# Local attention with its scores in eight 64x32 tiles of the array, one score and one transpose stage per tile, and outputs normalised instead of probabilities

## The chip, the cores and the metric

The kernel runs on one core of one Trainium2 chip. The metric is the device time of one execution in microseconds (us), as the median of several executions. A core has five engines that run side by side and wait for each other by semaphores: TensorE (PE in the profile; PEld is its loading of weights), VectorE (DVE), ScalarE (ACT), GpSimd (POOL) and SyncE (SP), which here only issues transfers. TensorE writes its products to PSUM, which has eight banks; everything else lies in SBUF.

## The reference

Four batches of eight heads hold 512 local and 32 global tokens of 64 numbers each. A local query sees the 32 global keys and the local keys at most 32 places away. Two feed-forward layers follow, over all 2176 tokens of 512 numbers:

```python
s_ll = np.where(np.abs(pos[:, None] - pos[None, :]) <= 32, scale * q_l @ k_l.T, -1e9)
s_lg = scale * q_l @ k_g.T
a_l = softmax(concatenate([s_lg, s_ll], -1))       # e / (sum(e) + 1e-9), e = exp(s - max)
out_l = a_l @ concatenate([v_g, v_l])
out_g = softmax(scale * q_g @ concatenate([k_g, k_l]).T) @ concatenate([v_g, v_l])
x = concatenate([out_g, out_l])                     # as (2176, 512)
x = (h * clip(h + 3, 0, 6) / 6) @ w_out             # h = x @ w_in, d_ff = 2048; float64 weights
x = elu(x @ w_in2) @ w_out2                         # the same sizes
```

## The kernel before, in words

**Products.** The tokens are 17 tiles of 128: 16 of local queries and one that holds all global ones. They are handled in six chunks of 3, 3, 3, 2, 3 and 3 tiles (`CHUNKS`). For each chunk and each of 16 slots of 128 of d_ff there is an `up` product (12 matmuls into one bank `h`) and, two slots later, a `down` product in two parts (6 and 6 matmuls into the four banks `acc`). Every operand is a high and a low part (`gh` and `gl`, `x1h` and `x1l`), so a product is three matmuls. After `up`, ScalarE and VectorE make `g` out of `h` (L403, L404), ScalarE rounds it to `gh` (L409), and `gl` is the rest (L411, on GpSimd in the first chunk and on VectorE afterwards).

**Weights.** They come as float64, seen as two words. `Split` turns a slot `f` into two float32 parts: L100 on ScalarE, L104, L108 and L111 on VectorE, L121 on ScalarE, and two subtractions on GpSimd (L123). For the first layer this happens at the start and during the first chunk, for the second layer during the last chunk of the first. `tick` spreads these stages: two calls in a step of a slot, the first with L104 and L121 and L123, the second with L108, L111 and L100.

**Local attention.** `Local` does one tile of 128 queries and all eight heads in six stages: scores of two pairs of heads (S of part 0 and of part 1), transposes of the probabilities (T of part 0 and of part 1), the values (O) and the transposes of the output (XT). In S a matmul takes the queries of two heads, 32 of each, as 64 columns over all 128 rows of the array; the other head's rows hold zeros. VectorE adds the mask and takes the minimum of the negated scores (L218), ScalarE takes the exponential with a running sum (L222), VectorE adds 1e-9 to the sums and inverts them (L225, L226), and the probabilities are multiplied by that (L229): on VectorE for the first three tiles, on GpSimd for the others. T goes through PSUM and ScalarE (L239); O is 32 matmuls of 32 columns each, and ScalarE copies it to `x` (L256). XT is turned into `x1h` (L263, ScalarE) and `x1l` (L264, VectorE). `Global` does 32 global queries of four heads in three stages (SG; TG with Tg; OG).

**Order.** It is written out by hand, and every engine works off its own queue in that order. The attention of the first three tiles stands ahead of all products, mixed with loads and splitting by the string `PRO`. The tiles of chunk c+1 are done during chunk c, in the gaps between its products: three gaps in a step (after `up`, and after either part of `down`). `place` gives the stages of a job their places and `step` the distance to the next job; `during` spreads them over the gaps. All stages after the first three tiles use two PSUM banks (`att`) in turn: a stage waits until the one that used its bank two turns earlier has been read out.

**Transfers.** SyncE issues all of them in one queue. A load waits at the queue's head until its buffer is free: `qk` has one buffer, so the next tile's queries and keys are loaded after the scores, and the values `v` (two halves with tag `v`) after O. The raw weights share 16 buffers (tag `w`) with the operands of the first three tiles and the finished weights.

Of the kernel before, what the change touches and what calls it, by code (L numbers as in the profile page):

```python
# [14 lines left out]
ALU = mybir.AluOpType  # L15
# [27 lines left out]
# A float64's upper word, read as float32, has the upper 8 of its 11 exponent bits as its exponent;  # L43
# times this it has them less 896 = 1023 - 127.
# [9 lines left out]
def tile_kernel(ctx, tc, qkW, vW, qkG, vN, vG, masks, w1, w2, out):  # L54
# [10 lines left out]
    msk = pool.tile([P, 3, 2, P], F32, name="msk")  # L65
# [63 lines left out]
    def tick(m, times=1):  # L129
        """The next two stages of splitting the weights of layer m, of slots that follow each other."""  # L130
# [28 lines left out]
    class Local:  # L159
        """Attention of 128 local queries, all heads, cut into stages."""  # L160

        def __init__(self, n):
# [3 lines left out]
            self.p = {}  # L166

        def load_qk(self):
            tag, bufs = ("w", NF) if self.early else ("qk", 1)
            qk = pool.tile([P, 2, 2, 2 * P + WIN], F32, name=f"qk{self.n}", tag=tag, bufs=bufs)  # L170
# [10 lines left out]
        def load_v(self):  # L181
# [6 lines left out]
            for i in range(2):  # L188
                nc.sync.dma_start(self.v[i], src[:, i])
# [471 lines left out]
```

## Time and profile before

| what | value |
|---|---|
| runs | 923.87, 925.02 and 925.42 us, median 925.02 us |
| profiled execution | span 923.7 us; the profile has no other time for it |
| PE busy | 883.6 us (96%) |
| PEld, DVE, ACT, POOL busy | 811.8, 411.6, 424.1 and 183.6 us |
| the chain that ended last | PE 80%, DVE 10%, ACT 5%, issue 4%, POOL 1% |
| moved | 90.27 MB, mean 98 GB/s |

The busy times are sums over stages of different kinds, so they don't tell what ends a given stage; the chain follows the work back from the last instruction, at each step to what released it. "Issue" in it is time for which the profile shows no wait.

### The profile page before, as it was taken

How to read it: one execution, taken by the hardware profiler on the slowest of the kernel's cores; microseconds unless marked ns; L12 is line 12 of the kernel's file. 1: busy time of each engine (PE TensorE's matmuls, PEld its weight loads, DVE VectorE, ACT ScalarE, POOL GpSimd, SP SyncE). 2: the span in 40 equal slices, each digit the busy share in tenths (PEclk: the TensorE clock that was granted, in tenths of full speed). 3: DMA queues.
4: the chain of work that ended last, by engine and by line, in shares of the span. 5: the costliest groups of instructions: out<-in, count | busy, mean ns of one | idle time of the engine just before them, and what ended most of it. 6: DMA issues, size and time to landing. Idle time of an engine off the chain costs nothing.

```text
span 923.7 us, 15740 instructions
## 1 busy us (share of the span) xinstructions
PE 883.6 (96%) x6432; PEld 811.8 (88%) x6432; DVE 411.6 (45%) x911; ACT 424.1 (46%) x944; POOL 183.6 (20%) x124
## 2 busy tenths in 40 slices
PE   6588799999999999999999989999999999999998
PEld 4477799989989999999999979999999999989997
DVE  4988864332432343432339978432222232322222
ACT  5666645433532354443335566533443444434433
POOL 0489781100100010000006644300100101001000
PEclk9799899999999999999999989999999999999999
DMA  9766313331423235232056630020010020100100
GB/s 371 319 270 225 135 47 109 131 122 45 134 80 130 65 124 164 89 101 67 1 179 238 259 140 18 18 69 0 1 57 1 1 69 1 57 1 1 35 1 34
DMA packets 21816, 90.27 MB, mean 98 GB/s; under 512 B 2544, under 2 KB 5872, under 8 KB 17264
## 3 DMA queue, kind: packets, MB, share of 16 engines
q1 hardware_dynamic: 21744, 89.27, 27.1%
q8 instruction: 50, 0.82, 0.4%
q14 instruction: 22, 0.18, 0.1%
HBM read 80.35 MB, written 8.91 MB: 97 GB/s over the span
## 4 chain that ended last, share of the span: by engine, by line
PE 80%; DVE 10%; ACT 5%; issue 4%; POOL 1%; DMA 0%; ACTq 0%; DVEq 0%
PE acc L389 36%; PE h L389 36%; DVE f L108 4%; DVE f L111 3%; PE S L204 3%; DVE f L104 1%; PE O L248 1%; PE T L74 1%; DVE g L404 1%; ACT P L222 1%; PE SG L316 1%; ACT room L222 1%; PE OG L346 1%; ACT w L121 1%; ACT gh L409 0%
## 5 line engine op out<-in xcount | busy, mean ns | idle before, releaser
L389 PE MATMUL acc<-gh,w 128*128 128x384 f32 (+1 forms) x768 | 213.9, 337 | 0.0
L389 PE MATMUL h<-x1h,w 128*128 128x384 f32 (+1 forms) x768 | 209.6, 338 | 4.0 <-POOL w L123 2.8
L389 PE MATMUL h<-x2h,w 128*128 128x384 f32 (+1 forms) x768 | 203.5, 330 | 0.0
L389 PE MATMUL acc<-w,gh 128*128 128x512 f32 x544 | 171.9, 397 | 3.3 <-ACT ev L437 3.3
L409 ACT CAST gh<-g 128x384 fp32r<-128x384 f32 (+1 forms) x192 | 95.1, 495 | 153.9 <-DVE g L404 90.9
L389 PEld LDWEIGHTS h<-x1h,w 128*128 128x128 f32 x768 | 140.0, 191 | 10.1 <-POOL w L123 3.5
L389 PEld LDWEIGHTS acc<-gh,w 128*128 128x128 f32 x768 | 139.3, 189 | 5.0 <-issue 3.8
L389 PEld LDWEIGHTS h<-x2h,w 128*128 128x128 f32 x768 | 138.7, 189 | 4.1
L408 DVE SCALAR_TENSOR_TENSOR g<-g,h 128x384 f32<-128x384 f32 (+1 forms) x96 | 51.1, 532 | 199.2 <-ACT g L407 199.2
L389 PE MATMUL h<-x1l,w 128*128 128x384 f32 (+1 forms) x384 | 127.6, 332 | 4.5 <-DVE x1l L264 4.5
L411 DVE TENSOR_TENSOR gl<-g,gh 128x384 fp32r<-128x384 f32 (+1 forms) x176 | 95.6, 543 | 77.1 <-ACT gh L409 77.0
L389 PE MATMUL acc<-gl,w 128*128 128x384 f32 (+1 forms) x384 | 126.9, 330 | 2.6 <-POOL gl L411 2.6
L123 POOL TENSOR_TENSOR w<-f,w 128x512 fp32r<-128x512 f32 x64 | 110.9, 1753 | 89.7 <-ACT w L121 89.7
L389 PE MATMUL h<-x2l,w 128*128 128x384 f32 (+1 forms) x384 | 126.7, 330 | 0.0
L404 DVE SCALAR_TENSOR_TENSOR g<-g,h 128x384 f32<-128x384 f32 (+1 forms) x96 | 50.9, 530 | 154.7 <-ACT g L403 154.6
L389 PEld LDWEIGHTS acc<-w,gh 128*128 128x128 f32 x544 | 101.1, 190 | 19.4 <-ACT ev L437 3.6
L406 ACT ACTIVATE g<-h 128x384 f32<-128x384 f32 (+1 forms) x96 | 45.5, 474 | 145.2 <-PE h L389 145.2
L403 ACT ACTIVATE g<-h,half 128x384 f32<-128x384 f32 (+1 forms) x96 | 53.9, 562 | 119.2 <-PE h L389 116.5
L389 PE MATMUL acc<-w,gl 128*128 128x512 f32 x272 | 108.1, 398 | 0.0
L464 POOL TENSOR_TENSOR x2l<-x2raw,x2h 128x768 fp32r<-128x768 f32 (+1 forms) x12 | 21.9, 1823 | 325.2 <-ACT x2h L463 325.2
L229 POOL TENSOR_TENSOR P<-P,sums 128x512 f32<-128x512 f32 x26 | 31.2, 1198 | 246.0 <-DVE sums L226 221.3
L389 PEld LDWEIGHTS h<-x1l,w 128*128 128x128 f32 x384 | 73.3, 191 | 4.9 <-DVE x1l L264 4.9
(72 smaller groups left out, 918.8 us busy)
## 6 DMA issues: line engine op xcount, KB each, us to landing
raw<-in_w SPq DMA_DIRECT2D x32, 1024.0 KB, 6.7
qk<-in_qkW SPq DMA_DIRECT2D x15, 960.0 KB, 4.8
v<-in_vW SPq DMA_DIRECT2D x26, 512.0 KB, 4.9
qkG<-in_qkG SPq DMA_DIRECT2D x8, 608.0 KB, 3.8
vN<-in_vN SPq DMA_DIRECT2D x8, 512.0 KB, 4.7
out<-ev SPq DMA_DIRECT2D x16, 256.0 KB, 2.1
x2d<-ev SPq DMA_DIRECT2D x20, 192.0 KB, 2.1
x2raw<-x2d SPq DMA_DIRECT2D x10, 384.0 KB, 3.7
```

The source lines that it names most:

```text
L108: nc.vector.scalar_tensor_tensor(w, self.high[:, s], -0x80000000, w, op0=ALU.bitwise_and, op1=ALU.bitwise_or)
L111: nc.vector.scalar_tensor_tensor(w, self.low[:, s], 29, w, op0=ALU.logical_shift_right, op1=ALU.bitwise_or)
L123: nc.gpsimd.tensor_sub(lo[:, i], self.wf[:, i], hi[:, i].bitcast(F32))
L204: nc.tensor.matmul(sp[r : r + 64, j, i // 2, :], self.q[:, part, j, i, :], self.k[:, part, j, 32 * i : 32 * i + P], start=True, stop=True,)
L229: eng.tensor_tensor(pf, pf, sums.unsqueeze(2).to_broadcast([P, 4, P]), op=ALU.mult)
L389: nc.tensor.matmul(o, a, b, start=first and i == 0, stop=last and i == len(pairs) - 1)
L403: nc.scalar.activation(g, hp, AF.Relu, scale=1.0 / 6.0, bias=half)
L404: nc.vector.scalar_tensor_tensor(g, g, 1.0, hp, op0=ALU.min, op1=ALU.mult)
L406: nc.scalar.activation(g, hp, AF.Relu, scale=-1.0)
L408: nc.vector.scalar_tensor_tensor(g, g, -1.0, hp, op0=ALU.add, op1=ALU.max)
L409: nc.scalar.copy(gh, g)
L411: late.append(lambda: eng.tensor_sub(gl, g, gh.bitcast(F32)))
```

## The change

`Local` is rebuilt. In S each head has its own matmuls: its 64 rows of the array (upper or lower half) by 32 columns, for 32 queries, so that eight such tiles of the array can be filled; the outputs of the upper half go to one bank (`S_0`) and those of the lower half to another (`S_1`). The zeros between the heads are gone from the transfer of the queries, and the mask is half as large. A tile has one S stage with 32 matmuls over two banks, one T stage with eight transposes over two banks, O over two banks, and XT: four stages in place of six. V has a 65th column of ones, so the last column of O is the sum of the probabilities; the sums of L222 and the multiplications of L229 (L numbers of before) are gone, and VectorE takes the sums out of O (L235 of the changed kernel), inverts them (L236) and multiplies the outputs (L239), which replaces ScalarE's copy of O. The operands and probabilities of later tiles have one buffer each, the places are 0, 4, 6, 8 with a step of 9 (before 0, 2, 4, 7, 9, 11 with a step of 6), those of `Global` 0, 3, 5 (before 0, 4, 8), and `PRO` has a new order. The diff, cut to its core:

```diff
--- before.py
+++ after.py
-PRO = "q0 q1 v0 q2 v1 00 01 10 02 11 03 20 v2 12 04 13 21 05 W4 14 a100 a200 a101 W a201 a300 15 22 a110 a111 a301 a400 a210 a211 a310 23 w1 24 a311 a401 w1 q3 25 a410 a411 w1 w1 w1 | W | | | | | w1 w1 | w1 | w1 v3 |"
+PRO = "q0 q1 v0 q2 v1 00 v2 10 01 W4 20 11 02 a100 a200 a101 W a201 a300 21 03 12 a110 a111 a301 a400 a210 a211 a310 13 22 w1 23 a311 a401 w1 q3 a410 a411 w1 w1 w1 | W | | | | | w1 w1 | w1 | w1 v3 |"
...
     class Local:
...
         def __init__(self, n):
...
         def load_qk(self):
...
+            qk = pool.tile([P, NP, P + WIN], F32, name=f"qk{self.n}", tag=tag, bufs=bufs)
...
+                nc.sync.dma_start(qk[:, :2], src[:, :2])
...
+                nc.sync.dma_start(qk[:, 2:], src[:, 2:])
...
+            self.q, self.k = qk[:, :, :P], qk[:, :, P:]
...
         def load_v(self):
...
+            tag, bufs = ("w", NF) if self.early else ("vw", 1)
+            self.v = pool.tile([P, TPB, H, D + 1], F32, name=f"v{self.n}", tag=tag, bufs=bufs)
+            nc.sync.dma_start(self.v, vW[self.b, self.t])
+        def buffers(self):
...
+                room = pool.tile([P, 2, 2, NP, P], F32, name=f"room{self.n}", tag="w", bufs=NF)
+                return room[:, 0], room[:, 1]
+            p = pool.tile([P, 2, NP, P], F32, name=f"P{self.n}", tag="p", bufs=1)
+            pt = pool.tile([P, 2, NP, P], F32, name=f"PT{self.n}", tag="pt", bufs=1)
+            return p, pt
+        def scores(self, tag):
+            self.p, self.pt = self.buffers()
+            sp = [bank([P, NP, P], f"S{self.n}_{r}", tag) for r in range(2)]
+            mn = pool.tile([P, 2, NP], F32, name=f"mn{self.n}", tag="mn", bufs=2)
+            mi = 0 if self.t == 0 else (2 if self.t == TPB - 1 else 1)
+            for j in range(NP):
                 for i in range(4):
...
+                    for r in range(2):
+                        rs, cs = slice(64 * r, 64 * r + 64), slice(32 * i, 32 * i + 32)
+                        nc.tensor.matmul(
+                            sp[r][cs, j, :], self.q[rs, j, cs], self.k[rs, j, 32 * i : 32 * i + P],
+                            start=True, stop=True,
+                        )
+            for j in range(NP):
+                for r in range(2):
                     nc.vector.tensor_tensor_reduce(
...
+                        out=self.p[:, r, j, :], in0=sp[r][:, j, :], in1=msk[:, mi, :], scale=-SCALE, scalar=BIG,
+                        op0=ALU.add, op1=ALU.min, accum_out=mn[:, r, j : j + 1],
...
                     nc.scalar.activation(
...
+                        self.p[:, r, j, :], self.p[:, r, j, :], AF.Exp, scale=-1.0, bias=mn[:, r, j : j + 1]
...
+        def transposed(self, tag):
+            for r in range(2):
+                tp = bank([P, NP, P], f"T{self.n}_{r}", tag)
+                for j in range(NP):
+                    transpose(tp[:, j, :], self.p[:, r, j, :])
+                nc.scalar.copy(self.pt[:, r], tp)
+        def values(self, tag):
+            op = [bank([P, NP, D + 1], f"O{self.n}_{r}", tag) for r in range(2)]
+            sums = pool.tile([P, 2, NP], F32, name=f"sums{self.n}", tag="sums", bufs=2)
+            for r in range(2):
+                for j in range(NP):
+                    for i in range(4):
+                        cs = slice(32 * i, 32 * i + 32)
+                        nc.tensor.matmul(
+                            op[r][cs, j, :], self.pt[:, r, j, cs], self.v[:, i, 2 * j + r, :], start=True, stop=True
+                        )
+                nc.vector.tensor_scalar_add(sums[:, r], op[r][:, :, D], 1e-9)
             nc.vector.reciprocal(sums, sums)
...
+            self.x = pool.tile([P, NP, 2, D], F32, name=f"x{self.n}", tag="x", bufs=1)
+            for r in range(2):
+                nc.vector.tensor_tensor(
+                    self.x[:, :, r, :], op[r][:, :, :D], sums[:, r].unsqueeze(2).to_broadcast([P, NP, D]), op=ALU.mult
+                )
...
         def turned(self, tag):
...
+                transpose(xp[:, kd, :], self.x[:, kd].rearrange("p r d -> p (r d)"))
...
+        def stages(self, tags=("att",) * 4, nxt=None):
             def first():
...
+                self.scores(tags[0])
...
+            def third():
+                self.values(tags[2])
...
+            return [first, lambda: self.transposed(tags[1]), third, lambda: self.turned(tags[3])]
...
     class Global:
...
         def __init__(self, b, hf):
...
-            self.v = pool.tile([P, TPB, 4, D], F32, name=f"vN{g}", tag="v", bufs=2)
+            self.v = pool.tile([P, TPB, 4, D], F32, name=f"vN{g}", tag="vw", bufs=1)
-            self.p = pool.tile([P, S], F32, name=f"PG{self.g}", tag="p", bufs=2)
+            self.p = pool.tile([P, S], F32, name=f"PG{self.g}", tag="p", bufs=1)
...
-            self.pt = pool.tile([P, TPB, P], F32, name=f"PTG{self.g}", tag="pt", bufs=2)
+            self.pt = pool.tile([P, TPB, P], F32, name=f"PTG{self.g}", tag="pt", bufs=1)
...
-            place, step = ((0, 2, 4, 7, 9, 11), 6) if isinstance(job, Local) else ((0, 4, 8), 6)
+            place, step = ((0, 4, 6, 8), 9) if isinstance(job, Local) else ((0, 3, 5), 6)
-        first = [locs[n].stages(tags=("acc", "acc", "att", "att", "h", "h")) for n in range(CHUNKS[0])]
+        first = [locs[n].stages(tags=("acc", "att", "h", "acc")) for n in range(CHUNKS[0])]
...
-    qb = np.zeros((B, TPB, 2, D, NP, 4, 2, 32), q_l.dtype)
...
+    qb = q_l.reshape(B, NP, 2, TPB, P, D).transpose(0, 3, 2, 5, 1, 4).reshape(B, TPB, P, NP, P)
...
-    vW = c(vw.transpose(0, 3, 5, 1, 4, 2, 6))
...
+    vW = np.ones((B, TPB, P, TPB, H, D + 1), v_l.dtype)
+    vW[..., :D] = vw.transpose(0, 2, 4, 3, 1, 5)
```

On PE, in the second chunk, names are `h_<chunk>_<slot>` for `up`, `acc_<chunk>_<bank>` for `down`; here is the stretch from XT of one tile to S of another, before:

```order
L74 MATMUL XT_1735<-ident,x_1709 128x128 x4
L389 MATMUL h_1_5_1744<-x1h_907,w_5_631 128x384
...
L389 MATMUL h_1_5_1744<-x1h_907,w_5_631 128x384
L389 MATMUL acc_1_0_1554<-gh_1_3_1607,w_3_543 128x384
...
L389 MATMUL acc_1_1_1555<-gh_1_3_1607,w_3_543 128x384
L204 MATMUL S_0_1770<-qk_1649 64x128 x8
L389 MATMUL acc_1_2_1556<-gh_1_3_1607,w_3_543 128x384
```

and the stretch from XT of the first tile of that chunk's attention to S of the second in the changed kernel:

```order
L365 MATMUL h_1_3_1689<-x1h_789,w_3_589 128x384
L74 MATMUL XT_1708<-ident,x_1667 128x128 x4
L365 MATMUL acc_1_0_1673<-gh_1_1_1568,w_1_470 128x384
...
L365 MATMUL acc_1_1_1674<-gh_1_1_1568,w_1_470 128x384
L203 MATMUL S_0_1726<-qk_1539 32x128
L203 MATMUL S_1_1727<-qk_1539 32x128
...
L365 MATMUL acc_1_2_1675<-gh_1_1_1568,w_1_470 128x384
```

Between XT and the following S there stood 18 matmuls of the products (12 of `up`, 6 of `down`), and now stand 6; XT itself now comes directly behind `up`, and S uses two banks, of which `S_1` is the one that XT has just filled.

On DVE, in the first chunk, `f` is a slot being split and `g_0_<slot>` the activation; here are the instructions of one step before:

```order
L404 SCALAR_TENSOR_TENSOR g_0_5_739<-g_0_5_739,h_0_5_726 128x384
L104 TENSOR_SCALAR f_8_724<-f_8_724 128x1024
L218 ISA P_1_768,mn_1_769<-S_1_759,msk 128x128
L218 ISA mn_1_769 128x1
...
L225 TENSOR_SCALAR sums_1_770<-sums_1_770 128x4
L226 RECIPROCAL sums_1_770<-sums_1_770 128x4
L108 SCALAR_TENSOR_TENSOR f_8_724<-raw_8_571,f_8_724 128x1024
L111 SCALAR_TENSOR_TENSOR f_8_724<-raw_8_571,f_8_724 128x1024
```

and in the changed kernel the steps with S of the same tile, and with O of the tile ahead of it:

```order
L380 SCALAR_TENSOR_TENSOR g_0_5_810<-g_0_5_810,h_0_5_797 128x384
L104 TENSOR_SCALAR f_8_795<-f_8_795 128x1024
L209 ISA P_830,mn_834<-S_0_832,msk 128x128
...
L108 SCALAR_TENSOR_TENSOR f_8_795<-raw_8_617,f_8_795 128x1024
...
L104 TENSOR_SCALAR f_6_637<-f_6_637 128x1024
L235 TENSOR_SCALAR sums_700<-O_0_698 128x4
L235 TENSOR_SCALAR sums_700<-O_1_699 128x4
L236 RECIPROCAL sums_700<-sums_700 128x8
L239 TENSOR_TENSOR x_736<-O_0_698,sums_700 128x4x64
L239 TENSOR_TENSOR x_736<-O_1_699,sums_700 128x4x64
L108 SCALAR_TENSOR_TENSOR f_6_637<-raw_6_509,f_6_637 128x1024
```

The instruction on the sums, which stood between the scores and L108 of a slot and needs ScalarE's exponentials, has left that place; in its stead the sums and the multiplications stand behind O, ahead of L108 of another slot.

On SP, `raw_0_<slot>` is a slot's float64 weights; here is the queue around the second later tile's values, before:

```order
L83 DMA raw_9_629<-in_w 128x2048
L83 DMA raw_10_695<-in_w 128x2048
L83 DMA raw_11_745<-in_w 128x2048
L177 DMA qk_782<-in_qkW 128x1920
L189 DMA v_0_825<-in_vW 128x1024
L189 DMA v_1_826<-in_vW 128x1024
L83 DMA raw_12_852<-in_w 128x2048
```

and now:

```order
L83 DMA raw_9_678<-in_w 128x2048
L183 DMA v_739<-in_vW 128x2080
L83 DMA raw_10_764<-in_w 128x2048
L83 DMA raw_11_816<-in_w 128x2048
L177 DMA qk_883<-in_qkW 128x1408
L83 DMA raw_12_914<-in_w 128x2048
```

The values, whose load waits for O of the tile before, moved ahead of slots 10 and 11.

## Rows read from the trace of the kernel before

**Rows 1.** Busy time by stretch: span, engines (instructions), clock, DMA share, GB/s.

```profile
0.00:26.50 26.50, 15.98 (x254) 13.01 (x255) 12.46 (x69) 15.65 (x59) 0.70 (x6) 0.94 0.94 377
26.50:130.50 104.00, 82.46 (x721) 73.97 (x720) 90.54 (x131) 62.99 (x128) 81.80 (x50) 0.92 0.55 207
130.50:483.40 352.90, 351.87 (x3216) 328.87 (x3217) 125.28 (x442) 147.89 (x395) 28.64 (x26) 1.00 0.30 99
483.40:541.70 58.30, 54.98 (x314) 54.66 (x312) 53.53 (x53) 34.77 (x50) 34.19 (x19) 0.99 0.64 231
541.70:923.70 382.00, 378.27 (x1932) 341.32 (x1932) 129.80 (x217) 162.77 (x316) 38.26 (x24) 0.99 0.08 27
```

**Rows 2.** Waits of PE, 130.6 to 483.4: total us, times, longest.

```profile
PE XT L74 <- ACT PTG L335: 0.8, 1, 0.8
```

**Rows 3.** The chain that ended last, in order of time: start, us, engine, line.

```profile
136.94 2.11 PE h L389 x12
139.04 1.02 PE S L204 x16
140.07 2.31 PE acc L389 x12
...
147.82 0.44 PE T L74 x4
148.26 2.10 PE h L389 x12
...
161.68 1.03 PE O L248 x64
162.71 1.25 PE acc L389 x6
...
168.00 1.05 PE acc L389 x6
```

**Rows 4.** Waits of DVE, 44.5 to 128.4: total us, times, longest.

```profile
DVE sums L225 <- ACT P L222: 8.2, 6, 2.1
DVE x1l L264 <- ACT x1h L263: 2.3, 2, 1.3
```

**Rows 5.** DVE and POOL by line, 44.5 to 128.4: busy us, mean ns | idle before.

```profile
L226 DVE RECIPROCAL sums<-sums 128x4 f32<-128x4 f32 x6 | 1.1, 178 | 0.2
...
L229 POOL TENSOR_TENSOR P<-P,sums 128x512 f32<-128x512 f32 x6 | 9.8, 1626 | 3.0 <-DVE sums L226 2.0 <-ACT g L403 1.0
```

**Rows 6.** DVE and POOL by line, 130 to 483: the same columns.

```profile
L218 DVE CUSTOM_DVE_ANT_0 P<-S,msk 128x128 f32<-128x128 f32 x80 | 18.5, 287 | 5.5 <-PE S L204 5.4
...
L404 DVE SCALAR_TENSOR_TENSOR g<-g,h 128x256 f32<-128x256 f32 x16 | 6.7, 421 | 25.1 <-ACT g L403 25.1
...
L229 POOL TENSOR_TENSOR P<-P,sums 128x512 f32<-128x512 f32 x20 | 21.4, 1070 | 242.9 <-DVE sums L226 219.3 <-ACT PT L239 17.9 <-ACT x L256 4.2
```

**Rows 7.** Timeline of DVE and POOL: start, us, engine, line.

```profile
41.24 1.23 DVE L108 SCALAR_TENSOR_TENSOR f<-raw,f 128x1024 int32<-128x1024 int32 x1
92.84 1.88 DVE L108 SCALAR_TENSOR_TENSOR f<-raw,f 128x1024 int32<-128x1024 int32 x1
94.76 1.95 DVE L111 SCALAR_TENSOR_TENSOR f<-raw,f 128x1024 int32<-128x1024 int32 x1
...
93.60 2.03 POOL L229 TENSOR_TENSOR P<-P,sums 128x512 f32<-128x512 f32 x1
```

**Rows 8.** XT of 197.57 and its readers: chain, ACT and DVE timelines.

```profile
197.57 0.44 PE XT L74 x4
...
199.29 0.58 ACT L263 CAST x1h<-XT 128x512 fp32r<-128x512 f32 x1
...
199.90 0.69 DVE L264 TENSOR_TENSOR x1l<-XT,x1h 128x512 fp32r<-128x512 f32 x1 [1.07 <-ACT x1h L263]
```

**Rows 9.** Waits of DVE, 0 to 26, and transfers: KB each, median us to landing.

```profile
DVE sums L225 <- ACT room L222: 6.7, 6, 1.1
...
raw<-in_w SPq DMA_DIRECT2D x32, 1024.0 KB, 6.7
```

More of the change, by code (lines that the diff above doesn't have):

```diff
@@ L64, in tile_kernel @@
     ident = pool.tile([P, P], F32, name="ident")
-    msk = pool.tile([P, 3, 2, P], F32, name="msk")
+    msk = pool.tile([P, 3, P], F32, name="msk")
     half = pool.tile([P, 1], F32, name="half")
@@ L191, in buffer @@
-        def buffer(self, name, tag, part):
-            if not self.early:
-                return pool.tile([P, 2, 2, P], F32, name=name, tag=tag, bufs=2)
-            if not self.p:
-                self.room = pool.tile([P, 4, 2, 2, P], F32, name=f"room{self.n}", tag="w", bufs=NF)
-            return self.room[:, 2 * (tag == "pt") + part]
-        def scores(self, part, tag):
-            sp = bank([P, 2, 2, P], f"S{self.n}_{part}", tag)
-            for j in range(2):
-                for i in range(4):
-                    r = i % 2 * 64
-                    nc.tensor.matmul(
-                        sp[r : r + 64, j, i // 2, :],
-                        self.q[:, part, j, i, :],
-                        self.k[:, part, j, 32 * i : 32 * i + P],
-                        start=True,
-                        stop=True,
-                    )
-            p = self.buffer(f"P{self.n}_{part}", "p", part)
-            mn = pool.tile([P, 4], F32, name=f"mn{self.n}_{part}", tag="mn", bufs=2)
-            sums = pool.tile([P, 4], F32, name=f"sums{self.n}_{part}", tag="sums", bufs=2)
-            mi = 0 if self.t == 0 else (2 if self.t == TPB - 1 else 1)
-            for j in range(2):
-                for hf in range(2):
-                    c = slice(2 * j + hf, 2 * j + hf + 1)
@@ L224, in scores @@
                     )
-            nc.vector.tensor_scalar_add(sums, sums, 1e-9)
-            nc.vector.reciprocal(sums, sums)
-            eng = nc.vector if self.early else nc.gpsimd
-            pf = p.rearrange("p j f k -> p (j f) k")
-            eng.tensor_tensor(pf, pf, sums.unsqueeze(2).to_broadcast([P, 4, P]), op=ALU.mult)
-            self.p[part] = p
-        def transposed(self, part, tag):
-            p = self.p[part]
-            tp = bank([P, 2, 2, P], f"T{self.n}_{part}", tag)
-            for j in range(2):
-                for hf in range(2):
-                    transpose(tp[:, j, hf, :], p[:, j, hf, :])
-            pt = self.buffer(f"PT{self.n}_{part}", "pt", part)
-            nc.scalar.copy(pt, tp)
-            self.p[part] = pt
@@ L242, in values @@
-        def values(self, tag):
-            op = bank([P, H, D], f"O{self.n}", tag)
-            for h in range(H):
-                pr, r = h // 2, 32 * (h % 2)
-                for i in range(4):
-                    c = i % 2 * 64 + r
-                    nc.tensor.matmul(
-                        op[32 * i : 32 * i + 32, h, :],
-                        self.p[pr // 2][:, pr % 2, i // 2, c : c + 32],
-                        (self.v[:, h // 4] if self.early else self.v[h // 4])[:, i, h % 4, :],
-                        start=True,
-                        stop=True,
-                    )
-            self.x = pool.tile([P, H, D], F32, name=f"x{self.n}", tag="x", bufs=1)
-            nc.scalar.copy(self.x, op)
+        def transposed(self, tag):
[4 more added lines that the diff above has]
+                nc.scalar.copy(self.pt[:, r], tp)
@@ L576, in _masks @@
 def _masks():
-    m = np.full((2, 2, 32, 3, 2, 4, 32), -1.0e9 / SCALE, np.float32)
+    m = np.full((4, 32, 3, 4, 32), -1.0e9 / SCALE, np.float32)
     order = [0, 1, 2, "g", 3, 4, 5]
@@ L584, in _masks @@
                 lb = order[i + w]
-                blk = m[i % 2, :, :, kind, i // 2, w, :]
+                blk = m[i, :, kind, w, :]
                 if lb == "g":
```

43 lines of the change are left out of this document (4 added, 39 removed).

## The prediction

> **What bounds the kernel now.** I read the busy time by stretch first, since the page's 96% for PE is a mean over stages of different kinds. [rows 1] has five stretches. From 541.7 on, PE is busy nearly all the time and no attention is left; between 483.4 and 541.7 VectorE is busy for 53.5 of 58.3 us, with the splitting of the second layer's weights. The change touches neither. From 130.5 to 483.4 PE is busy for 351.9 of 352.9 us and its waits are next to nothing, the longest 0.8 us [rows 2]: whatever the attention of ten tiles takes on PE there is paid in full, and no other engine matters until it makes PE wait. From 26.5 to 130.5 it is the other way round: VectorE is busy for 90.5 of 104 us, PE for 82.5. This is the first layer's splitting with the attention of three more tiles in it. VectorE works its queue in order, so its own waits count there: 8.2 us ahead of L225, the addition to the sums, which waits for ScalarE's exponentials, and 2.3 us ahead of L264 [rows 4]. The first 26.5 us are the attention of three tiles while the transfers run at 94% of their share; VectorE is busy for 12.5 us and waits 6.7 us for exponentials [rows 9].
>
> The price of attention on PE I read from the chain of work in order of time [rows 3]. An S stage takes 1.02 us for its 16 records (a matmul of this type leaves two), and the 12 matmuls behind it take 2.31 us where they take 2.11 otherwise, so 0.20 more go to coming back from a narrower tile of the array. T and XT take 0.44 us each (XT in [rows 8]) and nothing afterwards. O takes 1.03 us, and again 0.20 (six matmuls behind it 1.25 against 1.05). A tile costs 2 x 1.22 + 2 x 0.44 + 1.23 + 0.44 = 4.99 us.
>
> **The change, stretch 130.5 to 483.4.** O has 64 records in 1.03 us, S has 16 in 1.02. With a fixed part of 0.17 us in both that is 13.4 ns for a record of 64 columns on a quarter of the array and 53 ns for one of 128 columns on half of it: both fit if a record takes two cycles for a column at 2.4 GHz and all tiles of the array run side by side (64 x 2 / 2.4 / 4 = 13.3; 128 x 2 / 2.4 / 2 = 53). The new S has 64 records of 128 columns on an eighth of the array. No row shows two halves of the rows at work together, so I bound it: all eight at once, 128 x 2 / 2.4 / 8 = 13.3 ns a record and 64 x 13.3 + 170 = 1.02 us; only the four column tiles at once, 26.7 ns and 1.88 us. I take 1.02, as O already keeps up that pace of records, so issuing them isn't the limit. T is 0.88 as before, O has a 65th column (+1.6%, 1.05), XT stays. A tile then costs 1.02 + 0.20 + 0.88 + 1.05 + 0.20 + 0.44 = 3.79 us, 1.20 less: **-12.0 us** over ten tiles, or -3.4 at the other bound.
>
> Against it stands a new wait. S now needs both `att` banks at once, and one of them is XT's. In [rows 8] XT starts right behind `up` at 197.57, but its reader on ScalarE stands behind `gh`, so that L263 starts at 199.29, and L264 ends at 200.59, 3.0 us after XT's start. Where XT stands behind `up` and six matmuls of `down` lie between it and S (the first pair of tiles of the second chunk), S comes up after 0.44 + 1.05 = 1.5 us and PE waits 1.5. Where twelve lie between (2.11 us: one pair each in the third and fifth chunk), or XT comes after the first part of `down` (one pair in the second), it waits about 0.5 each. In the fourth chunk more products lie between. Together **+3.0 us**, between 0 (bank free in time) and 3.0. Behind the waiting S stand only products, whose operands are two slots ahead. The Trainium skill has a rule against this kind of edit ("TensorEngine Tiling (Array Packing)", section "PSUM Bottleneck"): tiles speed up the array but not the reading out of PSUM, which may become the bottleneck. By that rule, taken as an estimate, S would go at the pace of its eight reductions L218, 8 x 0.287 = 2.3 us for 1.02 [rows 6], and the sum would be some 13 us higher; but the reductions run beside the products that follow, so I keep the 3.0 us.
>
> The other edits cost nothing here: VectorE and ScalarE are busy for 125 and 148 of 353 us [rows 1], the multiplications on VectorE (six instructions a tile less on GpSimd and ScalarE, two more on VectorE) lie under the products between O and XT, at least 2.3 us; without that cover each pair would cost 0.8. Values of 16 KB more a tile lie in transfers at 30% share.
>
> **Stretch 44.5 to 128.4 (first chunk, VectorE).** (a) The wait of 8.2 us ahead of L225 goes, since the sums come out of O: -8.2. (b) Additions stay at two a tile, inversions go from six to three, at 0.18 [rows 5]: -0.5. (c) Six multiplications of 128x256 out of PSUM come to VectorE; the nearest row is L404 of the same size, 0.42 [rows 6]: +2.5. (d) GpSimd loses six L229, 9.8 us of it [rows 5], and VectorE's splitting is slower beside them: L108 takes 1.23 us alone and 1.88 at 92.84, L111 1.95 at 94.76, while an L229 ran from 93.60 to 95.63 [rows 7]. That is 1.4 us for this L229 and some of the instruction ahead of it, about 1.0 for L229; I count four of the six as lying on splitting: -4, between 0 and 6 x 1.07 = -6.4 (its length beside the products [rows 6]). (e) New waits: VectorE now waits for O of one tile (the one in the third gap of its step; the other two come early enough) and for x1h three times instead of twice, 1.2 us each by [rows 4]: 3.6 + 1.3 against 2.3, about +2.4, between -2.3 (no wait is left) and +8.2 (as long as the old ones). Sum **-7.8 us**, between -14.9 and +2.0. PE has the room: it is idle for 21.5 of the 104 us from 26.5 on [rows 1].
>
> For (d) the Trainium skill has a rule ("SBUF — State Buffer", section "Who interferes with whom"): a VectorE instruction with two SBUF inputs and a GpSimd one that reads SBUF exclude each other, and the second to start blocks until the first is done. By the rule all six would give back their full length and the sum would be 2.4 us lower; the rows show less than the full length (1.4 us against 2.03).
>
> On SP, slots 10 and 11 now queue behind the values that wait for O of the tile before. O of that tile stands in slot 3's step and slot 10 is first read in slot 6's, so three steps lie between, some 15 us (an estimate: the 104 us hold about 16 to 20 steps), against 6.7 for a landing [rows 9]: nothing, while each microsecond beyond would be one of VectorE's.
>
> **First 44.5 us.** Queries shrink from 960 to 704 KB a tile, the mask by 192 KB, values grow by 16: 912 KB less ahead of the first weights, 2.5 us at 377 GB/s [rows 1]. VectorE's work shrinks by about as much (L229 of three tiles to half-width multiplications), and the 6.7 us of waits [rows 9] go, but the splitting can't begin before the weights have landed. I take **-3 us**, by the transfers, between 0 and 6.7 + 2.5 = -9.2.
>
> **Sum.** -3.0 - 7.8 - 12.0 + 3.0 = -19.8: a span of 923.7 - 19.8 = 903.9 us. The median of the runs lies 1.3 us above the profiled span: 905.
>
> **Rivals.** (1) The two halves of the rows don't run together: S is 1.88 us, 8.6 us less is gained, 914. For it: no row shows them together. Against it: columns do in every row. (2) The first 128 us give nothing, since the waits only move from the exponentials to O and XT, in the same queue: about 10 us less, 915. For it: PE reaches O only behind products that wait for weights, for which it is idle now. Against it: one of three O stands where VectorE would wait. (3) The start and (d), (e) come out near their good ends: -8 and -12 for -10.8, 896. (4) Slower: the new tiles of the array take turns. A record alone needs 128 x 2 / 2.4 = 107 ns, S 64 x 107 = 6.8 us + 0.37, a tile 9.8 us, ten tiles +48 + 3; with -10.8 from the start, 923.7 + 40 = 964, so about 965 measured. It decides from an S of 3.0 us on (89 ns a matmul for the 27 that I take). For it: only the absence of a row; against it: O, whose four tiles share the array.
>
> **How the numbers follow.** Forecast 0.50, rivals (1) 0.18, (2) 0.15, (3) 0.10, (4) 0.05, and (1) with (2), close to no change, 0.02. The predicted time is 905. The range reaches from rival (3) to beyond (1) and (2), with some room for their sizes: 893 to 918. Half of the last 0.02 I give to slower: faster by over 0.2% (about what a measurement of this kernel can tell from no change) 0.93, within 0.2% 0.01, slower 0.06. The likeliest alone, with its terms' middle halves, reaches from 900 to 910.
>
> **What would show it.** S records 13 to 14 ns apart in the chain, a whole S near 1.0 us (step 1; 1.9 and 7 are the rivals); waits of S for L264's successor of up to 1.5 us, at four places; no wait of VectorE for the exponentials, short ones for O and XT in the first chunk; the last L111 about 11 us earlier; L108 and L111 nearer 1.2 us. The stretches of the second layer must keep their lengths. The prediction is wrong if the narrow tiles of the array hinder each other, if O or slot 10's weights hold up VectorE in the first chunk, or if PE waits for T's probabilities or O's, which I take to be ready in time.

## The result, and the profile after

The changed kernel takes 909.08 us (median; 908.02 to 910.19) where the one before takes 924.44 on the same chip: a ratio of 0.9834, 95% interval 0.9821 to 0.9848, so 15.4 us are gained. 905 was predicted, 893 to 918 as the range. The profiled execution has a span of 906.1 us (923.7 before), 17.6 us less.

The busy time by stretch, cut where those of [rows 1] are cut by their place in the work (first splitting, first product of the second chunk, splitting of the second layer's weights); the columns are the same:

```profile
0.00:21.50 21.50, 12.04 (x348) 9.45 (x348) 6.59 (x55) 11.22 (x31) 0.70 (x6) 1.00 0.90 351
21.50:125.70 104.20, 82.16 (x817) 73.73 (x817) 94.67 (x146) 59.80 (x101) 77.54 (x44) 0.89 0.56 212
125.70:468.20 342.50, 340.66 (x3539) 321.61 (x3538) 129.06 (x452) 133.01 (x305) 7.18 (x6) 1.00 0.28 96
468.20:525.80 57.60, 54.51 (x312) 54.18 (x311) 52.93 (x53) 33.99 (x48) 34.16 (x19) 1.00 0.65 233
525.80:906.10 380.30, 374.93 (x1932) 337.93 (x1932) 131.94 (x217) 163.21 (x318) 38.40 (x24) 1.00 0.08 27
```

The first stretch is 5.0 us shorter, the second not shorter at all (104.2 for 104.0), the third 10.4. To see where the gain comes and goes, marks in the work serve better than cuts. Timelines of VectorE, ScalarE and GpSimd, first of before, then of after: start of the first conversion of weights (L100), first g, last instruction of the first layer's splitting (L111), first instruction of the second layer's (L104), last L123.

```profile
25.25 1.26 ACT L100 ACTIVATE f<-raw 128x512 f32<-128x512 f32 x2
44.61 0.54 DVE L404 SCALAR_TENSOR_TENSOR g<-g,h 128x384 f32<-128x384 f32 x1
126.12 2.20 DVE L111 SCALAR_TENSOR_TENSOR f<-raw,f 128x1024 int32<-128x1024 int32 x1
482.09 0.69 DVE L104 TENSOR_SCALAR f<-f 128x1024 int32<-128x1024 int32 x1 [0.48 <-ACT f L100]
584.13 2.55 POOL L123 TENSOR_TENSOR w<-f,w 128x512 fp32r<-128x512 f32 x2 [4.84 <-ACT w L121]
```

```profile
20.80 1.22 ACT L100 ACTIVATE f<-raw 128x512 f32<-128x512 f32 x2 [2.70 <-DMA raw<-in_w]
45.45 0.54 DVE L380 SCALAR_TENSOR_TENSOR g<-g,h 128x384 f32<-128x384 f32 x1
120.31 1.91 DVE L111 SCALAR_TENSOR_TENSOR f<-raw,f 128x1024 int32<-128x1024 int32 x1
466.86 0.69 DVE L104 TENSOR_SCALAR f<-f 128x1024 int32<-128x1024 int32 x1 [0.49 <-ACT f L100]
568.18 2.56 POOL L123 TENSOR_TENSOR w<-f,w 128x512 fp32r<-128x512 f32 x2 [4.90 <-ACT w L121]
```

With the first product of the second chunk (136.94 in [rows 3], 132.17 in the chain below) the 17.6 us divide so:

| part | before | after | difference | predicted |
|---|---|---|---|---|
| start to first g | 44.61 | 45.45 | +0.8 | -3.0 |
| first g to first product of the second chunk | 92.33 | 86.72 | -5.6 | -7.8 |
| from there to the second layer's splitting | 345.15 | 334.69 | -10.5 | -12.0 + 3.0 |
| from there to the last L123 | 102.04 | 101.32 | -0.7 | 0 |
| from there to the end | 339.57 | 337.92 | -1.7 | 0 |

The last two rows hold nothing that the change touches; in the last stretch the granted clock was 0.99 before [rows 1] and 1.00 after, and that the 2.4 us of both rows come from it is not shown. Without them it is 15.2 us, near the 15.4 of the medians. The chain of work, in order of time, for the third part:

```profile
132.17 2.08 PE h L365 x12
134.25 1.09 PE S L203 x64
135.34 2.29 PE acc L365 x12
...
140.78 0.87 PE T L74 x8
...
144.83 1.05 PE O L232 x61
...
152.59 0.70 DVE x1l L249
153.34 1.14 PE S L203 x62
```

The new S takes 1.09 us for 64 records, and the 12 matmuls behind it 2.29, so 0.2 for the way back from narrow tiles, as before. In the last lines S starts only behind L249, the subtraction that frees XT's bank. The waits of PE from 125.8 to 468.2 (total us, times, longest):

```profile
PE S L203 <- DVE x1l L249: 1.8, 4, 1.3
```

Four places, as predicted, but 1.8 us for 3.0. VectorE from the first g to the end of the last L111 (with the L111 that the first g follows), by line (busy us, mean ns, then idle before), first lines of before, then lines of after:

```profile
L111 DVE SCALAR_TENSOR_TENSOR f<-raw,f 128x1024 int32<-128x1024 int32 x13 | 27.7, 2133 | 0.5
L108 DVE SCALAR_TENSOR_TENSOR f<-raw,f 128x1024 int32<-128x1024 int32 x12 | 19.9, 1661 | 0.3
L104 DVE TENSOR_SCALAR f<-f 128x1024 int32<-128x1024 int32 x12 | 12.1, 1006 | 0.0
...
L225 DVE TENSOR_SCALAR sums<-sums 128x4 f32<-128x4 f32 x6 | 2.3, 382 | 8.2 <-ACT P L222 8.2
```

```profile
L111 DVE SCALAR_TENSOR_TENSOR f<-raw,f 128x1024 int32<-128x1024 int32 x13 | 27.0, 2075 | 0.4
L108 DVE SCALAR_TENSOR_TENSOR f<-raw,f 128x1024 int32<-128x1024 int32 x12 | 20.4, 1698 | 0.2
L104 DVE TENSOR_SCALAR f<-f 128x1024 int32<-128x1024 int32 x12 | 12.8, 1067 | 0.0
L380 DVE SCALAR_TENSOR_TENSOR g<-g,h 128x384 f32<-128x384 f32 x14 | 7.6, 544 | 2.3 <-ACT g L379 2.3
...
L239 DVE TENSOR_TENSOR x<-O,sums 128x256 f32<-128x256 f32 x4 | 1.5, 418 | 0.1
L249 DVE TENSOR_TENSOR x1l<-XT,x1h 128x512 fp32r<-128x512 f32 x2 | 1.4, 692 | 2.1 <-ACT x1h L248 2.1
L235 DVE TENSOR_SCALAR sums<-O 128x4 f32<-128x4 f32 x4 | 0.4, 147 | 0.0
```

The wait of 8.2 us for the exponentials [rows 4] is gone, waits of 4.4 us stand for 2.3 (2.1 for x1h as before, and 2.3 of g for ScalarE, a wait that before had none of), and splitting takes 60.2 us for 59.7, although the six multiplications of GpSimd [rows 5] are gone too. From first g to the last L111's end it is 83.7 us before and 76.8 after, 6.9 less.

The first stretch lost what it had. VectorE's timeline in the start of after (in brackets the idle time before, and its cause):

```profile
21.49 0.99 DVE L104 TENSOR_SCALAR f<-f 128x512 int32<-128x512 int32 x2 [3.93 <-ACT f L100]
...
23.73 0.68 DVE L249 TENSOR_TENSOR x1l<-XT,x1h 128x512 fp32r<-128x512 f32 x1
...
30.72 0.75 DVE L239 TENSOR_TENSOR x<-O,sums 128x256 f32<-128x256 f32 x2
33.30 0.69 DVE L249 TENSOR_TENSOR x1l<-XT,x1h 128x512 fp32r<-128x512 f32 x1 [1.83 <-ACT x1h L248]
33.91 1.77 DVE L108 SCALAR_TENSOR_TENSOR f<-raw,f 128x512 int32<-128x512 int32 x1
```

The first weights are converted 4.45 us earlier (20.80 for 25.25). Not all of that is the transfers: after, L100 waits for the landing; before, it didn't, for ScalarE was still busy with exponentials and copies. There the first weights landed 18.1 us after their issue at 4.75, at 22.9 (the transfers issued from 4 to 5.5 us, last column us to landing):

```profile
raw<-in_w SPq DMA_DIRECT2D x1, 1024.0 KB, 18.1
```

So the landing gained 2.1 us, near the 2.5 worked out, and ScalarE's shorter queue the other 2.4. But from L100 to the first g it is 24.65 us where it was 19.36: two tiles' normalising, one more subtraction and a wait of 1.83 us now stand amid the splitting, while VectorE idled 3.9 us for the weights just before.

### The profile page after: what moved, and what is told of

Read it like the earlier page. It is cut to its first block, busy times and chain, and to the rows that moved or that the text cites. A ratio compares the mean times of both kernels' runs of the same rounds, so it can differ in the third digit from the quotient of the medians.

```text
span 906.1 us, 16516 instructions
## 1 busy us (share of the span) xinstructions
PE 864.3 (95%) x6944; PEld 796.9 (88%) x6944; DVE 415.2 (46%) x921; ACT 401.2 (44%) x800; POOL 158.0 (17%) x98
## 4 chain that ended last, share of the span: by engine, by line
PE 77%; DVE 12%; ACT 4%; issue 3%; DMA 2%; POOL 1%; SPq 0%; ACTq 0%; DVEq 0%
PE acc L365 35%; PE h L365 35%; DVE f L108 5%; DVE f L111 3%; DMA raw<-in_w 2%; DVE f L104 1%; PE S L203 1%; PE O L232 1%; ACT w L121 1%; DVE g L380 1%; PE T L74 1%; PE SG L292 1%; PE OG L322 1%; DVE x1l L249 1%; ACT gh L385 1%
## 5 line engine op out<-in xcount | busy, mean ns | idle before, releaser
L365 PE MATMUL h<-x1h,w 128*128 128x384 f32 (+1 forms) x768 | 207.1, 334 | 5.7 <-DVE g L380 3.9
L123 POOL TENSOR_TENSOR w<-f,w 128x512 fp32r<-128x512 f32 x64 | 111.7, 1766 | 88.7 <-ACT w L121 88.7
L365 PE MATMUL h<-x2l,w 128*128 128x384 f32 (+1 forms) x384 | 125.8, 328 | 0.0
L365 PEld LDWEIGHTS acc<-gl,w 128*128 128x128 f32 x384 | 72.7, 189 | 7.5 <-POOL gl L387 7.5
L365 PEld LDWEIGHTS h<-x2l,w 128*128 128x128 f32 x384 | 72.2, 188 | 4.1
```

The lines of the kernel that those rows point to most:

```text
L123: nc.gpsimd.tensor_sub(lo[:, i], self.wf[:, i], hi[:, i].bitcast(F32))
L365: nc.tensor.matmul(o, a, b, start=first and i == 0, stop=last and i == len(pairs) - 1)
```

## The experiments

Theory: S gains because all eight tiles of the array work together, less its waits for XT's bank; in the first chunk VectorE still sets the pace and gains by normalising outputs; the start gains nothing because attention moved into the splitting. Rivals: TensorE's issue sets the pace of a record; TensorE, not VectorE, sets that of the first chunk. Times are medians; differences to the changed kernel are those of the ratios to the kernel before, times 924.4 us, since chips differ (each ratio's interval is some 1.2 us to either side; that a difference of two runs is then uncertain by some 1.7 us is an estimate from this). One number in two expectations is misread: 116.6 us, or 116.3 by its row, is the end of the last L111 but one, and the last ends at 122.2; the differences that they expect are taken from there.

**Row halves apart.**

```diff
-            for j in range(NP):
-                for i in range(4):
-                    for r in range(2):
+            for r in range(2):
+                for j in range(NP):
+                    for i in range(4):
```

> The 64 matmuls of S in another order: first all of one half of the array's rows, then all of the other; nothing else. Theory A (S is fast because neighbouring matmuls lie on different halves of the rows and run together): S goes from 0.86 to 1.09 us to about 1.8 us, 0.8 us a tile over the ten tiles from 131 to 466 us, the span +8 to +10, so 917 to 919 measured. Rival B (the pace of 13 ns is that at which matmuls are issued, whatever tiles of the array they use): S stays below 1.2 us and the time within 2 us of the 909.1 of the changed kernel.

911.02 us, ratio 0.9856 (0.9843 to 0.9870), 2.0 more. The chain's S:

```profile
134.70 1.49 PE S L203 x64
```

1.49 lies between both: alternating the halves is worth 0.40 us a tile, half of what A says. As nothing but the order changed, the halves do run together, at least in part. Over ten tiles that is 4.0 us; the waits for XT's bank fall from 1.8 to 0.6, since the first half needs only the other bank, and the third part of the table is 2.1 us longer. B holds for the time, just, but falls by S.

**Half of O's columns.**

```diff
-                            op[r][cs, j, :], self.pt[:, r, j, cs], self.v[:, i, 2 * j + r, :], start=True, stop=True
+                            op[r][cs, j, 32:], self.pt[:, r, j, cs], self.v[:, i, 2 * j + r, 32:], start=True, stop=True
```

> O is computed with 33 instead of 65 columns (half of the values' columns and the ones), and the half outputs are used twice; the output therefore isn't the reference's. Theory A, the prediction's reading (a record takes two cycles for a column and the tiles of the array run side by side: 13 ns for 65 columns on four tiles): O goes from 1.05 to about 0.6 us, ten tiles from 131 to 466 us are 4 to 5 us shorter, time 903.5 to 906. Rival B (13 ns is the pace at which TensorE takes up its next matmul, whatever its columns; then S couldn't have become shorter with yet more tiles either): O stays at 1.0 us or more, time 908 to 910.

906.13 us, ratio 0.9799 (0.9786 to 0.9813), 3.2 less. The chain's O:

```profile
145.98 0.69 PE O L232 x59
```

A, if with less than it says (0.6 us, 906): columns set the time. 32 columns less are 0.36 us less, 11.3 ns a column for the 64 records where the prediction's reading gives 64 x 2 / 2.4 / 4 = 13.3; the part that doesn't hang on columns is then 1.05 - 65 x 0.0113 = 0.32 us and not 0.17.

**Ten slots from one tile to the next.**

```diff
-            place, step = ((0, 4, 6, 8), 9) if isinstance(job, Local) else ((0, 3, 5), 6)
+            place, step = ((0, 4, 6, 8), 10) if isinstance(job, Local) else ((0, 3, 5), 6)
```

> The slots from one pair of tiles' stages to the next are 10 instead of 9, so that S of the next tile stands one slot behind XT of the tile before and not right behind its products. Theory A (S waits for the bank that XT's readers still hold): the waits of S on the subtraction L249, 3.1 us in sum from 120 to 466 us, go, and up to 3.5 us of such waits in the first chunk; time 903 to 907. Rival B (the bank is only late because the work behind it is late, and the wait goes to the products of the tile or to another instruction): S no longer waits but acc or h waits as long, time 908 to 910.

906.78 us, ratio 0.9811 (0.9797 to 0.9824), 2.1 less. PE's waits from 120 to 470 us:

```profile
PE S L203 <- DVE x1l L249: 0.6, 3, 0.2
PE acc L365 <- POOL gl L387: 0.2, 1, 0.2
```

A, if not in full: the wait fell from 1.8 to 0.6 us and nothing took its place; the third part is 333.1 us for 334.85 (from the first product's first matmul), so 0.5 us more than the wait explains. In the first chunk S's waits for XT's bank stayed at 3.5 us, so there the expectation was wrong; the prediction has none in that chunk.

**Probabilities normalised again** (cut to the core; O is then copied by ScalarE).

```diff
+            for r in range(2):
+                nc.vector.tensor_scalar_add(sums[:, r], sums[:, r], 1e-9)
+                nc.vector.reciprocal(sums[:, r], sums[:, r])
+                eng = nc.vector if self.early else nc.gpsimd
+                eng.tensor_tensor(
+                    self.p[:, r], self.p[:, r], sums[:, r].unsqueeze(2).to_broadcast([P, NP, P]), op=ALU.mult
+                )
...
-                nc.vector.tensor_tensor(
-                    self.x[:, :, r, :], op[r][:, :, :D], sums[:, r].unsqueeze(2).to_broadcast([P, NP, D]), op=ALU.mult
-                )
+                nc.scalar.copy(self.x[:, :, r, :], op[r][:, :, :D])
```

> The probabilities are normalised again as before the change: sums with the exponentials, addition and inversion on VectorE, multiplication on GpSimd (VectorE for the first three tiles), O copied by ScalarE; the tiles of the array and the single stages stay. It undoes one part of the change. Theory A (normalising outputs took 11 us of waits and of GpSimd off VectorE in the first chunk, but only 4.8 us of it reached TensorE, which is now held by other things there): the last L111 comes 8 to 12 us later than the 116.6 us of the changed kernel, yet the first product of the second chunk comes only 3 to 6 us later, time 912 to 915. Rival B (the gain of the first chunk is from fewer bytes and fewer instructions, not from where is normalised): time 908 to 911, the last L111 within 4 us.

919.14 us, ratio 0.9943 (0.9931 to 0.9956), 10.1 more, beyond both. The last L111 ends at 128.2 (122.2), 6.0 later and short of A's 8 to 12; the first product of the second chunk comes 4.6 later, as A says. The rest was expected by neither: the third part is 6.4 us longer (341.2 for 334.85). PE's T there, with its idle time, first in the changed kernel, then in this run:

```profile
L74 PE MATMUL T<-ident,P 128*128 128x128 f32 x80 | 10.4, 272 | 0.0
L74 PE MATMUL T<-ident,P 128*128 128x128 f32 x80 | 11.8, 279 | 4.5 <-POOL P L222 4.4
```

With one S a tile all eight reductions, eight exponentials and two multiplications stand between S and T, and four slots don't cover them: T waits 4.4 us in sum for GpSimd, and takes 11.8 us for 10.4. So normalising outputs isn't an edit that costs nothing beside the single stages: it is what makes them fit.

Two more things stand in this trace. The six multiplications on GpSimd lengthen the first chunk's splitting from 58.0 us (60.2 without the L111 that the first g follows) to 62.5:

```profile
L111 DVE SCALAR_TENSOR_TENSOR f<-raw,f 128x1024 int32<-128x1024 int32 x12 | 25.9, 2157 | 0.4
L108 DVE SCALAR_TENSOR_TENSOR f<-raw,f 128x1024 int32<-128x1024 int32 x12 | 21.8, 1814 | 0.3
L104 DVE TENSOR_SCALAR f<-f 128x1024 int32<-128x1024 int32 x12 | 14.8, 1237 | 0.0
```

And the first g comes at 44.27, 1.2 us earlier than in the changed kernel, with the same order of the start: there, normalising outputs costs time.

**Two idle multiplications on GpSimd.**

```diff
+            if CHUNKS[0] <= self.n < CHUNKS[0] + CHUNKS[1]:
+                for r in range(2):
+                    idle = pool.tile([P, NP, P], F32, name=f"idle{self.n}_{r}", tag="idle", bufs=1)
+                    nc.gpsimd.tensor_tensor(idle, self.p[:, r], self.p[:, r], op=ALU.mult)
```

> Two multiplications of 128x512 a tile come back to GpSimd for the three tiles of the first chunk's stretch, reading the probabilities; nobody reads their output. It costs GpSimd about 6 x 1.6 us. Theory A, the prediction's own term (a GpSimd instruction that reads SBUF slows the splitting on VectorE by about 1 us): the last L111 comes 4 to 6 us later than 116.6 and L108 and L111 get longer in the mean by 0.1 us or more. Rival B (VectorE's splitting always runs beside some GpSimd work and keeps its mean): L108 and L111 within 0.05 us of 1.61 and 2.09, the last L111 within 1.5 us of 116.6; what gets later are the gl of GpSimd that stand behind, and TensorE's waits for them grow from 5.2 us; time 909 to 914.

913.50 us, ratio 0.9883 (0.9870 to 0.9897), 4.5 more. VectorE from first g to the last L111's end, and GpSimd's new line, from 40 to 121 us:

```profile
L111 DVE SCALAR_TENSOR_TENSOR f<-raw,f 128x1024 int32<-128x1024 int32 x13 | 27.4, 2108 | 0.4
L108 DVE SCALAR_TENSOR_TENSOR f<-raw,f 128x1024 int32<-128x1024 int32 x12 | 20.8, 1730 | 0.2
L104 DVE TENSOR_SCALAR f<-f 128x1024 int32<-128x1024 int32 x12 | 13.7, 1139 | 0.0
```

```profile
L219 POOL TENSOR_TENSOR idle<-P 128x512 f32<-128x512 f32 x6 | 9.1, 1522 | 2.3 <-ACT P L213 2.1
```

9.1 us on GpSimd cost the splitting 61.9 - 60.2 = 1.7 us, 0.3 an instruction, and that stretch 79.05 for 76.8 us. So there is such a cost, but not A's 1 us an instruction; the last L111 comes 2.8 us later, between A and B. Behind it another 1.5 us are lost up to the second chunk. This part is nearer to B, with another wait than it names: PE's waits for GpSimd's parts of the weights grow from 1.1 to 6.3 us, those for gl fall from 5.2 to 3.7. The lines of the changed kernel and of this run:

```profile
PE h L365 <- POOL w L123: 1.1, 2, 0.6
PE h L369 <- POOL w L123: 6.3, 3, 3.6
```

How the 4.5 us divide between the two engines, the run doesn't settle.

**The start's wait filled** (a piece of PRO, the order of the start).

```diff
-22 w1 23 a311 a401 w1
+22 w1 a311 23 a401 w1
```

> In the order of the start one stage changes places: the third tile's XT (stage 23) comes behind the stage of splitting that now follows it (a311), so that VectorE subtracts and shifts words of slot 1 between the multiplication L239 of this tile and its L249, which waits 1.83 us for ScalarE. Theory A (what the start saves in transfers, 4.5 us up to the first L111, is lost again because the third tile's attention with its waits now stands amid the splitting): the wait goes, the first g comes 1 to 2 us earlier, the time is 907.0 to 908.5. Rival B (TensorE's own work sets the start and the first chunk): the first g comes earlier, the first product of the second chunk doesn't, time 908.5 to 909.5.

907.70 us, ratio 0.9814 (0.9801 to 0.9827), 1.8 less. In the profiled execution the first weights happened to land 1.2 us later than in the changed kernel's (L100 at 21.97), so the first g comes at 45.43 as there, but 23.46 instead of 24.65 us behind L100:

```profile
34.60 0.69 DVE L249 TENSOR_TENSOR x1l<-XT,x1h 128x512 fp32r<-128x512 f32 x1 [0.50 <-ACT x1h L248]
```

The wait fell from 1.83 to 0.50 us, the way from L100 to g by 1.2, and the time by 1.8, little more than its uncertainty: A.

**A stage of splitting later** (one w1 from the first section to the third).

```diff
-a410 a411 w1 w1 w1 | W | | |
+a410 a411 w1 w1 | W | w1 | |
```

> The last stage of splitting ahead of the first product of two slots later moves behind that product's section, so that g of slot 0 stands ahead of two 2 us instructions of slot 3 on VectorE. Theory A (h of slot 2 waits 3.9 us for its bank, which that g reads, and the first chunk follows TensorE there): h of slot 2 comes 3 to 4 us earlier and the time is 905.5 to 908. Rival B (VectorE sets the pace of the whole first chunk; an earlier h of slot 2 only waits for the weights of slot 3 then): the last L111 stays within 1 us and the time is 908 to 911.

910.12 us, ratio 0.9843 (0.9830 to 0.9857), 0.8 more by the medians, within the intervals. Against L100 (at 21.69), h of slot 2 came 2.3 us earlier (44.60 for 46.04) and the last L111 ended 1.0 later (124.1 for 122.2): B. Shortening PE's wait of 3.9 us there gains nothing.

**All three, and two of them.** The first has the distance of 10, the filled wait and the later stage; the second leaves the later stage out. The edits are those above.

> The 10 slots' distance of the second run, the filled wait and the later stage of splitting together. If the waits that they remove lie on the path one behind the other: 2.3 us from the distance, 1.5 from the filled wait and 2 from the later stage, time 903 to 905. If VectorE's work sets the first chunk alone: only the distance counts, 906 to 908.

> The 10 slots' distance and the filled wait together, without the later stage of splitting. Both theories of the filled wait expect the distance's 2.3 us; if the filled wait is worth 1.2 us more on the path, 904.8 to 906.2, if it isn't, 906.3 to 907.5.

906.59 us, ratio 0.9806 (0.9792 to 0.9819), with the later stage; 904.95 us, ratio 0.9791 (0.9778 to 0.9804), without. The second is the fastest version of all, 4.0 us below the changed kernel, which is what its two parts give alone (2.1 + 1.8). The first comes out as if only the distance counted, but for another reason than expected: the later stage takes back what the filled wait gives. The times alone (1.4 us apart) don't show that; in the traces the second chunk begins 1.2 us later behind L100 with the later stage than without.

**Attention ahead of the splitting** (with the distance of 10; the first of the two with the filled wait too).

```diff
-W4 20 11 02 a100 a200 a101 W a201 a300 21 03 12 a110 a111
+W4 20 11 02 21 03 12 a100 a200 a101 W a201 a300 a110 a111
```

> As the run with the distance and the filled wait, and in the start T of the third tile, XT of the first and O of the second (stages 21 03 12) stand ahead of the first stages of splitting (a100 to a300). Theory A (VectorE waits 3.9 us for the first weights, with the subtraction of the first tile and the normalising of the second behind it, whose inputs lie ready): this work of 1.8 us and the chain behind it fit into the wait, the first g comes 1.5 to 2.5 us earlier and the time is 902.5 to 904.5. Rival B (the weights' transfers or TensorE set the first products, so that VectorE gets its work later elsewhere): within 1 us of the run with the distance and the filled wait.

905.09 us, ratio 0.9795 (0.9781 to 0.9808). VectorE's and ScalarE's timelines:

```profile
20.75 0.69 DVE L249 TENSOR_TENSOR x1l<-XT,x1h 128x512 fp32r<-128x512 f32 x1 [1.57 <-ACT x1h L248]
...
43.48 0.54 DVE L380 SCALAR_TENSOR_TENSOR g<-g,h 128x384 f32<-128x384 f32 x1
```

```profile
23.79 1.30 ACT L100 ACTIVATE f<-raw 128x512 f32<-128x512 f32 x2 [1.30 <-DMA raw<-in_w]
```

The first g is 0.6 us earlier than with the distance and the filled wait alone (44.09), not 1.5 to 2.5: part of the idle time became a wait for ScalarE of 1.57 us, and the next weights land late. Counted from L100 (21.28 for 20.95) it is 0.9 us. The time doesn't show it: by its number B, by the trace less than A expects.

> As the run before, with all stages of the three tiles (also 13, 22, 23) ahead of the first splitting. Theory A: chains of O, normalising, XT and subtraction, 3 to 4 us a tile, can't all lie in 3.9 us; VectorE starts splitting 2 to 3 us later but has no attention left in it, 902 to 905. Rival B: the later start of the splitting counts in full, the time is 1 to 3 us above that of the run with stages 21 03 12 alone.

906.96 us, ratio 0.9814 (0.9798 to 0.9829), 1.8 above: B, though the intervals of the two still overlap. L100 starts at 26.30, and the three subtractions wait 5.1 us for ScalarE.

## Why the prediction was right, and where not

**Third part (predicted -9.0, measured -10.5).** Right in its mechanism. The eight tiles run together, S 1.09 us for 1.02. By the chain a tile takes 1.09 + 0.20 + 0.87 + 1.05 + 0.20 + 0.44 = 3.85 us, 1.14 less than before. The bank's wait is 1.8 us for 3.0, and the ten slots, which take 1.2 of it away, shortened this part by 1.75. -11.4 + 1.8 makes -9.6; the 0.9 left to -10.5 is about the size of before's own waits (0.8 [rows 2] and 0.3 us), which are gone. What was mis-sized did not count: the other bound of S would have been 1.49 and not 1.88 us, so rival (1) was worth 4 us less than thought. What was missing is that the single S stage holds only because the outputs are normalised; "the other edits cost nothing here" hides 6.4 us that this edit avoids. Rival (4) falls with the 1.09.

S doesn't go at the pace of its eight reductions: they take 2.3 us and S 1.09, and PE waits nowhere for them. The Trainium skill's "TensorEngine Tiling (Array Packing)", section "PSUM Bottleneck", warns that reading PSUM may become the bottleneck of packed tiles; here the trace doesn't bear it out, as products lie between S and T. The nearest thing to it is the run with normalised probabilities, where T came too early for the chain behind S.

**First chunk (predicted -7.8; VectorE -6.9, of which PE took 5.6).** Near, but by terms that are wrong against each other, and that is luck. (a) -8.2 came in full. (d), the relief of splitting by -4, is the step that failed: splitting went from 59.7 to 60.2 us, and the signs that went with it, the last L111 11 us earlier and L108 near 1.2 us, failed too (6.1 us and 1.70). L229 did lie on the splitting: added up from the timelines of both engines, 8.2 of its 9.8 us ran beside it. But GpSimd's other work took its place. It was busy during 49.1 of the 57.5 us of splitting before and 51.4 of 58.0 after (here without the L111 ahead of the first g). With idle multiplications it was 56.6 of 59.7, with normalised probabilities 60.4 of 62.5: splitting gets longer as more of it runs beside GpSimd, whatever that does. So the price of a multiplication depends on where it falls, 0.3 us in one run and 0.75 in the other.

(d) was offset by L225 and L226, 3.4 us busy before, with 0.8 for what replaced them (b had -0.5): an addition took 382 ns before and 147 after, and the third tile's end now lies behind the last L111. For the same reason (c) is 1.5 and not 2.5 us. (e) comes out at 4.4 - 2.3 = +2.1 for +2.4, but not as foreseen: there is no wait for O and no more for x1h in this stretch (2.1 for 2.3), and 2.3 us are g's waits for ScalarE, which the prediction doesn't have.

VectorE stays the bound: moving work away from PE's wait there won nothing, undoing the normalisation lost all of it. "PE has the room" held for most: 1.3 us were lost between the last L111 and the second chunk.

By the Trainium skill's "SBUF — State Buffer", section "Who interferes with whom", VectorE's two-input instructions and GpSimd's would exclude each other; here VectorE lost 1.7 us of splitting for 9.1 us of idle GpSimd work added and 4.5 for the 9.1 us of normalising, both less than the rule's full length.

**First stretch (predicted -3, measured +0.8).** The step that failed, and outside its own bounds (0 to -9.2). The landing gained about what was worked out (2.1 for 2.5 us), but "the splitting can't begin before the weights have landed" was only half of it. Before, it began 2.4 us behind the landing, as ScalarE and VectorE were still at the attention, so the landing was no bound there. After, L100 does wait for the landing, but the changed order lets the second tile's normalising and the third tile's O and XT stand behind the first splitting, in VectorE's one queue. Then VectorE waits 3.9 us for weights with work behind it, and 1.8 us for ScalarE amid the splitting. Filling the second wait gave 1.2 us back on the path; using the first one gave 0.6 us at the first g and nothing measurable. So the start gives nothing, as rival (2) says for this part, though by other waits than it names.

In sum 3.8 + 2.2 us were missed and 1.5 us gained on top, 4.5 us in the first three parts. The last two rows took off 2.4, so the profiled span lies 2.2 us above the predicted 903.9. The rest of the 4.1 us between 905 and 909 is the step from span to median: 1.3 us were taken, and 3.0 were measured, as the profiled execution was the fastest of the four. That 905 came so near is in part this cancelling.

## What to carry to other kernels

On an engine that is never idle, a stage priced by its rows comes out (1.5 us off in 350 here); where an in-order queue is the bound, list what stands in it before and after, as a saved transfer or wait is worth only what the next instruction in that queue can use. When two stages become one, look at the chain behind it: moving the normalisation behind the product was what kept PE from waiting. A bank shared by two stages wanted one slot of distance more here than the products alone did: 2.1 us for one number.

## What was not expected of the hardware

With the two halves of the rows one after the other, S took 1.49 us for its 64 records, though O's rows (11.3 ns a column, 0.32 us besides) make 128 x 0.0113 + 0.32 = 1.77. Why 64 rows on four tiles run faster than 128 rows on four is open; no run tells. The conversion of the first weights began between 20.8 and 22.0 us in kernels with the same transfers up to there, each time behind the landing, so times in the start are best counted from there.
